# A Strassen tile and shared units of 128, 64 and 32 rows in a top-1 expert layer

## The chip, the cores and the metric

The kernel runs on one core of a Trainium2 chip. The metric is device time in microseconds (us), lower is better. Before the change it is 566.95 us, the median of 3 runs (565.99 to 568.38). The span in the profile, from the first to the last recorded instruction, is shorter (546.6 us), because the launch around it is not in the span.

## The reference

Two blocks follow one another: attention over a band of 96 keys and 8 global ones, and then a layer of 8 experts in which each token goes to the one expert with the highest logit. The change is in the second block alone.

```python
N, D, E, F = (3072, 512, 8, 1024)         # tokens, width, experts, hidden width

def _moe_ref(x, w_gate, w1, w2):
    logits = x @ w_gate
    expert_idx = np.argmax(logits, axis=1)
    ...                                   # gate_w: softmax weight of the chosen expert
    for e in range(E):
        mask = expert_idx == e
        xe = x[mask]
        h = np.maximum(xe @ w1[e], 0.0)   # (rows, 512) @ (512, 1024)
        ye = h @ w2[e]                    # (rows, 1024) @ (1024, 512)
        out[mask] = gate_w[mask, None] * ye
```

All is float32. On the reference's inputs the eight experts get 455, 416, 361, 397, 367, 410, 395 and 271 tokens.

## The kernel before

The attention block scatters each token's row to a region of its expert in DRAM (`xs_dram`); the counts are known only then. `P` is 128, `NDC` = 512/128 = 4, `NFC` = 1024/128 = 8. Every expert is computed in two pieces.

The first 128 rows of an expert are a fixed tile, of one shape for all (`x_in_s` turns the gathered rows with TensorE so that the width lies on the partitions):

```python
def up_s(self, e, half):
    ph = self.turn("ph")                  # a PSUM bank out of three, in turn
    for i in range(NFC // 2):
        f = half * (NFC // 2) + i
        for c in range(NDC):
            nc.tensor.matmul(ph[:, i, :], lhsT=self.w[e % 3][0][:, c, ts(f, P)],
                             rhs=self.xsT[e % 2][:, c, :], start=(c == 0), stop=(c == NDC - 1), ...)
    nc.scalar.activation(self.hsT[...], ph[...], AF.Relu)

def down_s(self, e, half):
    for f in range(half * (NFC // 2), (half + 1) * (NFC // 2)):
        nc.tensor.matmul(py, lhsT=self.hsT[:, f, :], rhs=self.w[e % 3][1][:, f, :], ...)   # 512 columns
    if half:
        nc.vector.tensor_scalar(self.ys[e % 2][:], py, self.gates[:, e:e + 1], None, ALU.mult)
        self.scatter(...)
```

The rows beyond 128 are a pass whose width `n` is a multiple of 16 up to 384. It is chosen by a computed jump (`tc.Switch`) among 18 bodies:

```python
TP = 3
GN = 16
WIDTHS = [0] + list(range(P, TP * P + 1, GN))

def one_pass(self, e, n, between):
    for f in range(NFC if n else 0):
        ph = self.turn("ph")...[:, 0:n]
        for c in range(NDC):
            nc.tensor.matmul(ph, lhsT=w1t[:, c, ts(f, P)], rhs=xT[:, c, 0:n], ...)
        nc.scalar.activation(hT[:, f, 0:n], ph, AF.Relu)
    other()                               # transposes of the next expert's rows
    for d in range(NDC if n else 0):
        py = self.turn("py")...[:, 0:n]
        for f in range(NFC):
            nc.tensor.matmul(py, lhsT=w2t[:, f, ts(d, P)], rhs=hT[:, f, 0:n], ...)
        nc.scalar.copy(self.yT[d % 2][:, 0:n], py)
        if d:
            self.back(e, d - 1, n)        # transposes y back to rows, VectorE scales by the gate
            other()

def passes(self, judge):
    for e in range(E):
        index = {eng: self.forms[e] for eng in self.ENGINES}     # PE, ACT, DVE jump
        for i in tc.Switch(index, len(WIDTHS), hint=f"pass{e}"):
            ...
            self.one_pass(e, WIDTHS[i], more)
        if e + 3 < E: self.fetch(e + 3)   # 4 MB of weights into one of three slots
        ...                               # gathers for later experts
        if e + 1 < E: self.hint(e + 1)    # hints for PE and ACT only (ENGINES[:2])
        ...                               # the fixed tile of expert e + 2, and finish(e)
```

For the eight experts the widths come out as 336, 288, 240, 272, 240, 288, 272 and 144.

Of the kernel before, what the change touches and what calls it, by code (L numbers as in the profile page):

```python
# [9 lines left out]
F32 = mybir.dt.float32  # L10
# [13 lines left out]
def kernel(  # L24
# [227 lines left out]
    def banded(stack, rt, pool, rows, ex, den_all):  # L252
# [195 lines left out]
        for n in range(N + 1):  # L448
# [8 lines left out]
            if n == 2:  # L457
                biases(0, range(H), "act")
                ex.clear_s()
# [271 lines left out]

    NS = 2
    TP = 3
    GN = 16
    WIDTHS = [0] + list(range(P, TP * P + 1, GN))

    class Experts:
        def __init__(self, stack, rt):
# [3 lines left out]
            self.w = [self.slot(self.wpool, i) for i in range(NS)]  # L742
            T = self.pool.tile
            self.pl = T([P, TP], F32, name="pl")
            self.lim = T([P, E], F32, name="lim")
            self.loc = T([P, E, TP], F32, name="loc")
            self.row = T([P, E, TP], F32, name="row")
            self.grow_s = T([P, E], I32, name="grow_s")
            self.inv_s = T([P, E], I32, name="inv_s")
            self.grow = T([P, E, TP], I32, name="grow")  # L750
            self.inv_i = T([P, E, TP], I32, name="inv_i")
            self.form = T([P, E], I32, name="form")
            self.over = T([P, 1], F32, name="over")
            self.xs = [T([P, XW], F32, name=f"xs{i}") for i in range(2)]
# [3 lines left out]
            self.tos = T([P, E], I32, name="tos")  # L758
            self.gates = T([P, E], F32, name="gates")

        def slot(self, pool, i):
            return pool.tile([P, NDC, F], F32, name=f"w1_{i}"), pool.tile([P, NFC, DM], F32, name=f"w2_{i}")

        def fetches(self, e, queue=nc.sync, parts=2):

            w1t, w2t = self.w[e % 3]
            for dst, src, n in ((w1t, moe_w1, NDC), (w2t, moe_w2, NFC)):
                s_ = src[e].rearrange("(c p) f -> p c f", p=P)
                for a in range(0, n, n // parts):
                    r = slice(a, a + n // parts)  # L770
                    yield lambda dst=dst, s_=s_, r=r: queue.dma_start(out=dst[:, r, :], in_=s_[:, r, :])

        def fetch(self, e, queue=nc.sync):
            for load in self.fetches(e, queue):
                load()
# [8 lines left out]
        def scatter(self, src, idx):  # L784
            d = nc.gpsimd.indirect_dma_start(  # L785
                out=out[:], out_offset=bass.IndirectOffsetOnAxis(ap=idx, axis=0),
                in_=src, in_offset=None, bounds_check=NTOK - 1, oob_is_err=False,
            )
            tc.declare_no_dep(d.ins, group="y", reason="every token is in one tile")
            tc.add_to_no_dep_group("y", d.ins)  # L790

        def clear_s(self):
            for t in self.xs:
                nc.gpsimd.memset(t[:], 0.0)
            nc.gpsimd.memset(self.lim[:], float(P))
            nc.gpsimd.iota(self.pl[:], pattern=[[P, TP]], base=0, channel_multiplier=1,
                           allow_small_or_imprecise_dtypes=True)


        def early(self):  # L800
            T = self.pool.tile
            cnt = T([P, NS], F32, name="cnt_s")
            nc.vector.tensor_tensor(cnt[:], self.rt.base_e[:, 0:NS], ebase[:, 0:NS], ALU.subtract)
            nc.vector.tensor_scalar(self.lim[:, 0:NS], cnt[:], float(P), None, ALU.min)
            self.rows_s(cnt, 0, NS)
            shape = [P, E, TP]
            nc.vector.tensor_tensor(self.loc[:], self.pl[:].unsqueeze(1).to_broadcast(shape),
                                    self.lim[:].unsqueeze(2).to_broadcast(shape), ALU.add)
            nc.vector.tensor_tensor(self.row[:], self.loc[:],
                                    ebase[:].unsqueeze(2).to_broadcast(shape), ALU.add)  # L810
            for e in range(NS):
                self.gather_s(e)

        def rows_s(self, cnt, a, b):
            n = b - a
            inv = self.pool.tile([P, n], F32, name=f"inv_s{a}")
            nc.vector.tensor_scalar(inv[:], cnt[:], iota_p[:, 0:1], None, ALU.is_le)
            row = self.pool.tile([P, n], F32, name=f"row_s{a}")
            nc.vector.tensor_scalar(row[:], ebase[:, a:b], iota_p[:, 0:1], None, ALU.add)
            nc.vector.scalar_tensor_tensor(self.grow_s[:, a:b], inv[:], float(2 ** 22), row[:],  # L820
                                           ALU.mult, ALU.add)
            nc.vector.tensor_scalar(self.inv_s[:, a:b], inv[:], float(2 ** 30), None, ALU.mult)

        def gather_s(self, e):
            self.gather(self.xs[e % 2][:], self.grow_s[:, e:e + 1])


        def x_in_s(self, e, pt=None):
            x, pt = self.xs[e % 2], pt or self.turn("t")
            for c in range(NDC):  # L830
                nc.tensor.transpose(pt[:, c, :], x[:, ts(c, P)], ident[:])
            nc.vector.tensor_copy(out=self.xsT[e % 2][:].rearrange("p c t -> p (c t)"),
                                  in_=pt[:].rearrange("p c t -> p (c t)"))
# [4 lines left out]
        def up_s(self, e, half):  # L838
            ph = self.turn("ph")
            for i in range(NFC // 2):  # L840
                f = half * (NFC // 2) + i
                for c in range(NDC):
                    nc.tensor.matmul(ph[:, i, :], lhsT=self.w[e % 3][0][:, c, ts(f, P)],  # L843
                                     rhs=self.xsT[e % 2][:, c, :], start=(c == 0), stop=(c == NDC - 1),
                                     skip_group_check=True)
            nc.scalar.activation(self.hsT[:, half * (NFC // 2):(half + 1) * (NFC // 2), :]
                                 .rearrange("p a b -> p (a b)"), ph[:].rearrange("p a b -> p (a b)"), AF.Relu)

        def down_s(self, e, half):
            if half == 0:  # L850
                self.pys = self.turn("py")
            py = self.pys[:].rearrange("p a b -> p (a b)")
            for f in range(half * (NFC // 2), (half + 1) * (NFC // 2)):
                nc.tensor.matmul(py, lhsT=self.hsT[:, f, :], rhs=self.w[e % 3][1][:, f, :],  # L854
                                 start=(f == 0), stop=(f == NFC - 1), skip_group_check=True)
            if half:
                nc.vector.tensor_scalar(self.ys[e % 2][:], py, self.gates[:, e:e + 1], None, ALU.mult)
                self.scatter(self.ys[e % 2][:], self.tos[:, e:e + 1])


        def begin(self, stack):

            pool = stack.enter_context(tc.tile_pool(name="pass", bufs=1, reuse_waits="tile"))
            self.w.append(self.slot(pool, NS))
            self.xg = [pool.tile([P, TP, XW], F32, name=f"xg{i}") for i in range(2)]
            self.xT = [pool.tile([P, NDC, TP * P], F32, name=f"xT{i}") for i in range(2)]
            self.hT = pool.tile([P, NFC, TP * P], F32, name="hT")
            self.yT = [pool.tile([P, TP * P], F32, name=f"yT{i}") for i in range(2)]
            self.y = [pool.tile([P, TP, DM], F32, name=f"y{i}") for i in range(2)]
            self.to = [pool.tile([P, TP], I32, name=f"to{i}") for i in range(2)]  # L870
            self.gate = [pool.tile([P, TP], F32, name=f"gate{i}") for i in range(2)]
            ps = stack.enter_context(tc.tile_pool(name="ps_e", bufs=1, space=bass.MemoryType.PSUM,
                                                 reuse_waits="tile"))
            self.bank = {nm: [ps.tile([P, 4, P], F32, name=f"{nm}{i}") for i in range(n)]
                         for nm, n in (("ph", 3), ("py", 2), ("t", 3))}
            self.used = {"ph": -1, "py": -1, "t": -1}

        def turn(self, nm):

            self.used[nm] += 1  # L880
            return self.bank[nm][self.used[nm] % len(self.bank[nm])]

        def clear(self, i):
            nc.gpsimd.memset(self.xg[i][:], 0.0)

        def clear_y(self):
            for i in range(2):
                nc.gpsimd.memset(self.y[i][:], 0.0)
                nc.gpsimd.memset(self.yT[i][:], 0.0)

        def table(self):
            T = self.pool.tile
            shape = [P, E, TP]
            cnt = T([P, E], F32, name="cnt")
            nc.vector.tensor_tensor(cnt[:], self.rt.base_e[:], ebase[:], ALU.subtract)
            inv = T(shape, F32, name="inv")
            nc.vector.tensor_tensor(inv[:], self.loc[:], cnt[:].unsqueeze(2).to_broadcast(shape), ALU.is_ge)
            nc.vector.scalar_tensor_tensor(self.grow[:], inv[:], float(2 ** 22), self.row[:],
                                           ALU.mult, ALU.add)
            nc.vector.tensor_scalar(self.inv_i[:], inv[:], float(2 ** 30), None, ALU.mult)  # L900
            self.rows_s(cnt[:, NS:E], NS, E)

            steps = T([P, E], F32, name="steps")
            nc.vector.scalar_tensor_tensor(steps[:], cnt[:], float(GN - 1), self.lim[:],
                                           ALU.add, ALU.subtract)
            steps_i = T([P, E], I32, name="steps_i")
            nc.vector.tensor_scalar(steps_i[:], steps[:], 0.0, None, ALU.max)
            nc.vector.tensor_scalar(steps_i[:], steps_i[:], GN.bit_length() - 1, None,
# [225 lines left out]
```

## Time and profile before

| | before |
|---|---|
| device time, median (range) | 566.95 us (565.99 to 568.38) |
| span in the profile | 546.6 us |
| TensorE (PE) busy | 518.6 us, 95% of the span |
| VectorE (DVE) busy | 170.5 us, 31% |
| ScalarE (ACT) busy | 127.3 us, 23% |
| GpSimd (POOL) busy | 113.9 us, 21% |
| first expert matmul starts | 168.69 us |
| last expert matmul ends | 529.56 us |

An engine's busy time is the time in which at least one of its instructions runs. A group of instructions is listed with its line, engine, operation, operands, shape and count, then busy time and the mean duration of one instruction. One float32 matmul of the program stands in the records as two matmul instructions: `one_pass` has 32 matmuls upwards for each of 8 experts, 256, and the profile counts 512. Matmuls overlap one another, so what one of them costs is read from the distance between starts, not from its duration. "idle" in square brackets is the time in which the engine waited before an instruction, and after the arrow stands what released it; "issue" is a wait for nothing that the profile shows.

### The profile page before, as it was taken

The page shows a single profiled execution, that of the slowest core. Times are in us where ns is not written, and L with a number is a line of the kernel's source. Part 1 is how long each engine was busy: PE and PEld are TensorE (multiplying, and loading weights), DVE is VectorE, ACT ScalarE, POOL GpSimd, SP SyncE. Part 2 cuts the span into 40 slices and gives each one's busy share as a digit, 9 for nine tenths or more (in the row PEclk, how much of TensorE's full clock was granted, in tenths as well). Part 3 has the DMA queues.
Part 4 walks back from the last instruction along what each step waited for, and adds up shares of the span by engine and source line. Part 5 has one row for each costly group of instructions (what it writes and reads, how often), then busy time and mean ns, then how long its engine had stood idle before and what let it go on. Part 6 is the DMA issues. An engine that isn't in the chain of part 4 may idle for free.

```text
span 546.6 us, 11060 instructions
## 1 busy us (share of the span) xinstructions
PE 518.6 (95%) x4544; PEld 428.3 (78%) x4544; DVE 170.5 (31%) x440; ACT 127.3 (23%) x249; POOL 113.9 (21%) x160
## 2 busy tenths in 40 slices
PE   5899999999999999999999999999999999999970
PEld 4798898898988756686787997789699886789940
DVE  5566866866866030110020211011002012011010
ACT  3644455554441001010100201111111210111200
POOL 4200240321334580014002202201400400201020
PEclk9999999999999999999999999999999999999995
DMA  9999999999941493353325246245344200100010
GB/s 173 211 201 207 243 270 240 241 306 240 240 147 40 143 342 112 152 178 113 107 82 189 57 156 214 63 155 177 102 155 154 68 1 7 64 1 31 17 45 7
DMA packets 98378, 77.22 MB, mean 141 GB/s; under 512 B 79290, under 2 KB 79290, under 8 KB 98240
## 3 DMA queue, kind: packets, MB, share of 16 engines
q1 hardware_dynamic: 88768, 52.44, 37.7%
q0 software_dynamic: 7040, 18.99, 10.1%
q10 hardware_dynamic: 2432, 4.21, 2.2%
q8 instruction: 55, 0.90, 0.7%
q14 instruction: 83, 0.68, 0.4%
HBM read 60.90 MB, written 14.73 MB: 138 GB/s over the span
## 4 chain that ended last, share of the span: by engine, by line
PE 73%; issue 18%; DVE 2%; ACT 2%; POOL 2%; DMA 1%; POOLq 0%; SPq 0%; ACTq 0%
PE ph L949 15%; PE py L956 14%; PE ph L843 9%; PE sp L358 8%; PE py L854 8%; PE po L387 7%; PE pt L239 4%; PE pr L398 4%; PE px L417 2%; PE t L927 1%; POOL out_dram L785 1%; DVE p L372 1%; PE pr L403 1%; PE t L970 1%; DMA raw_k<-in_k_dram 1%
## 5 line engine op out<-in xcount | busy, mean ns | idle before, releaser
L956 PE MATMUL py<-hT,w 128*128 128x288 f32 (+4 forms) x512 | 116.2, 383 | 0.0
L949 PE MATMUL ph<-xT,w 128*128 128x288 f32 (+4 forms) x512 | 113.9, 383 | 0.4 <-ACT hT L951 0.4
L949 PEld LDWEIGHTS ph<-xT,w 128*128 128x128 f32 x512 | 92.9, 190 | 22.0 <-issue 2.7
L956 PEld LDWEIGHTS py<-hT,w 128*128 128x128 f32 x512 | 91.5, 190 | 17.6
L973 DVE TENSOR_TENSOR y<-t,gate 128x256 f32<-128x256 f32 (+2 forms) x32 | 13.5, 421 | 148.9 <-PE t L970 106.1
L843 PE MATMUL ph<-xsT,w 128*128 128x128 f32 x512 | 59.7, 275 | 0.0
L843 PEld LDWEIGHTS ph<-xsT,w 128*128 128x128 f32 x512 | 58.4, 192 | 0.5 <-issue 0.5
L372 DVE TENSOR_TENSOR p<-sp,other 128x1024 f32<-128x1024 f32 x40 | 47.1, 1220 | 34.3 <-PE sp L358 32.4
L854 PE MATMUL py<-w,hsT 128*128 128x512 f32 x128 | 56.8, 592 | 0.0
L951 ACT ACTIVATE hT<-ph 128x288 f32<-128x288 f32 (+4 forms) x64 | 24.6, 388 | 130.5 <-PE ph L949 130.5
L785 POOL DMA_INDIRECT out_dram<-y,to x24 | 23.9, 995 | 141.4 <-DVE y L973 136.5
L928 DVE COPY xT<-t 128x512 f32<-128x512 f32 x24 | 15.6, 682 | 111.6 <-PE t L927 111.6
L379 ACT ACTIVATE p<-p 128x1024 f32<-128x1024 f32 (+1 forms) x48 | 44.6, 977 | 2.1 <-DVE p L372 2.0
L854 PEld LDWEIGHTS py<-w,hsT 128*128 128x128 f32 x128 | 23.5, 190 | 25.4 <-issue 25.3
L358 PE MATMUL sp<-qt,kt 64*128 64x128 f32 x448 | 39.0, 281 | 1.2 <-DVE kt L244 1.2
L958 ACT COPY yT<-py 128x288 f32<-128x288 f32 (+4 forms) x32 | 12.0, 376 | 113.5 <-PE py L956 113.5
L387 PE MATMUL po<-p,vt 128*64 128x128 f32 x448 | 37.1, 274 | 0.0
L358 PEld LDWEIGHTS sp<-qt,kt 64*128 64x128 f32 x448 | 31.9, 193 | 3.2 <-ACT qt L242 1.5
L778 POOL DMA_INDIRECT xs<-xs_dram,grow_s x8 | 8.1, 1009 | 118.1 <-issue 90.6
L219 POOL DMA_INDIRECT xs_dram<-xr,slot_i x24 | 23.7, 989 | 20.8 <-DVE base_e L217 9.8
L300 POOL COPY ka<-kt 128x384 f32<-128x384 f32 x16 | 8.2, 512 | 94.0 <-DVE den_all L423 90.9
L387 PEld LDWEIGHTS po<-p,vt 128*64 128x64 f32 x448 | 26.5, 137 | 1.3 <-ACT qt L242 1.2
(157 smaller groups left out, 508.0 us busy)
## 6 DMA issues: line engine op xcount, KB each, us to landing
w<-in_moe_w_dram SPq DMA_DIRECT2D x20, 1024.0 KB, 5.6
w<-in_moe_w_dram SPq DMA_DIRECT2D x16, 512.0 KB, 6.0
raw_q<-in_q_dram SPq DMA_DIRECT2D x24, 256.0 KB, 5.2
raw_k<-in_k_dram SPq DMA_DIRECT2D x24, 256.0 KB, 5.8
vt<-in_v_dram SPq DMA_DIRECT2D x24, 256.0 KB, 5.6
w<-in_moe_w_dram ACTq DMA_DIRECT2D x4, 1024.0 KB, 6.6
va<-vt SPq DMA_DIRECT2D x16, 192.0 KB, 5.6
va<-vt SPq DMA_DIRECT2D x16, 64.0 KB, 5.7
```

What stands on the lines that cost most here:

```text
L219: d = nc.gpsimd.indirect_dma_start(out=xs_dram[:], out_offset=bass.IndirectOffsetOnAxis(ap=slot_i[:, u:u + 1], axis=0), in_=xr[:, u, :].bi ...
L239: nc.tensor.transpose(pt[:, m, :], src[:, 2 * m:2 * m + 2, :].rearrange("p a d -> p (a d)"), ident[:])
L358: nc.tensor.matmul(sp[:, a, j, t, :], lhsT=kt[r, m, :], rhs=qts[n][r, m, :], start=True, stop=True, skip_group_check=True)
L372: nc.vector.tensor_tensor(z, sc, bi, ALU.add)
L379: nc.scalar.activation(z, z, AF.Exp)
L387: nc.tensor.matmul(po[D * a:D * a + D, m, :], lhsT=vt[:, 2 * m + a, :], rhs=ps[n][m // 2][:, a, m % 2, t, :], start=(x == 0), stop=(x == l ...
L785: d = nc.gpsimd.indirect_dma_start(out=out[:], out_offset=bass.IndirectOffsetOnAxis(ap=idx, axis=0), in_=src, in_offset=None, bounds_check ...
L843: nc.tensor.matmul(ph[:, i, :], lhsT=self.w[e % 3][0][:, c, ts(f, P)], rhs=self.xsT[e % 2][:, c, :], start=(c == 0), stop=(c == NDC - 1), ...
L854: nc.tensor.matmul(py, lhsT=self.hsT[:, f, :], rhs=self.w[e % 3][1][:, f, :], start=(f == 0), stop=(f == NFC - 1), skip_group_check=True)
L949: nc.tensor.matmul(ph, lhsT=w1t[:, c, ts(f, P)], rhs=xT[:, c, 0:n], start=(c == 0), stop=(c == NDC - 1), skip_group_check=True)
L951: nc.scalar.activation(hT[:, f, 0:n], ph, AF.Relu)
L956: nc.tensor.matmul(py, lhsT=w2t[:, f, ts(d, P)], rhs=hT[:, f, 0:n], start=(f == 0), stop=(f == NFC - 1), skip_group_check=True)
```

## The change

The work is cut in another way. Experts 0 and 1 keep a fixed tile of 128 rows, which runs while the routing table is made. Then every expert gets one tile of 256 rows. Each of its two products is cut into quarters and done by Strassen's scheme (in Winograd's form): seven products of quarters in place of eight, at the price of sums of quarters. What rows remain are done in units of 128, 64 and 32; the units that are needed are a number `k` from 0 to 7, bit by bit, and a computed jump chooses among 8 bodies. For the eight experts `k` comes out as 3, 1, 4, 5, 4, 5, 5 and 1. Units of 64 and 32 rows use only 64 or 32 columns of TensorE's array, and the kernel puts two or four such products side by side on different columns. The change is for fewer multiplications on TensorE.

The sums of quarters go to VectorE, those of w2 for the larger part to GpSimd, and the copies of half-done sums out of PSUM to ScalarE. Room for the sums comes from the third weight slot, so weights are now held for two experts instead of three, and those of expert e + 2 are fetched at the end of expert e. The down products now have the rows on the output's partitions, so y is no longer transposed back.

The core of the diff (declarations, the routing table and the transposes left out):

```diff
-    TP = 3
-    GN = 16
-    WIDTHS = [0] + list(range(P, TP * P + 1, GN))
+    SP1 = 32
+    FORMS = 8
+    HF = NFC // 2
+    HD = NDC // 2
+    HM = DM // 2
...
+        def combine1(self, e):           # four sums of quarters of w1, 128 x 1024 each
+            yield lambda: nc.vector.tensor_tensor(c[:, 0], a21, a22, ADD)
+            yield lambda: nc.vector.tensor_tensor(c[:, 1], c[:, 0], a11, SUB)
+            yield lambda: nc.vector.tensor_tensor(c[:, 2], a11, a21, SUB)
+            yield lambda: nc.vector.tensor_tensor(c[:, 3], a12, c[:, 1], SUB)
+        def combine_w2(self, e):         # four sums of quarters of w2, 128 x 1024 each
+            c = self.combine2(e)
+            c[2](nc.vector)
+            for i in (0, 1, 3):
+                c[i](nc.gpsimd)
+        def up_a(self, e, j):            # four products of quarters, 128 columns, into bank u[j]
+            for r, lhs, rhs in (...):
+                for k in range(HD):
+                    nc.tensor.matmul(self.u[j][:, r, :], lhsT=lhs(k), rhs=rhs(k), start=first, stop=True, ...)
+        def up_sums(self, j):
+            uv = self.uv[j]
+            nc.scalar.copy(uv[:], self.u[j][:, 0:2, :])
+            nc.vector.tensor_tensor(uv[:], uv[:], self.u[j][:, 2:4, :], ADD)
+            nc.vector.tensor_tensor(self.h[:, j, 3, :], uv[:, 0, :], uv[:, 1, :], ADD)
+            nc.scalar.activation(self.h[:, j, 3, :], self.h[:, j, 3, :], AF.Relu)
+        def up_b(self, e, j):            # the other three products, added into the same bank
+            for r, lhs, rhs in (...):
+                for k in range(HD):
+                    nc.tensor.matmul(self.u[j][:, r, :], lhsT=lhs(k), rhs=rhs(k), start=False, stop=True, ...)
+        def up_end(self, j):             # the hidden rows and the sums of their quarters
+            nc.vector.tensor_tensor(h[:, 1:3, :], ..., b[:, 1:4:2, :], ADD)
+            nc.vector.tensor_scalar(h[:, 0, :], b[:, 0, :], 0.0, None, MAX)
+            nc.scalar.activation(h[:, 2, :], h[:, 2, :], AF.Relu)
+            nc.vector.scalar_tensor_tensor(c[:, 0, :], h[:, 1, :], 0.0, h[:, 3, :], MAX, ADD)
+            nc.vector.tensor_tensor(c[:, 1, :], c[:, 0, :], h[:, 0, :], SUB)
+            nc.vector.scalar_tensor_tensor(c[:, 2, :], h[:, 1, :], 0.0, h[:, 0, :], MAX, SUB)
+            nc.vector.tensor_tensor(c[:, 3, :], h[:, 2, :], c[:, 1, :], SUB)
+        def units(self, e, k):           # the body number k of the jump
+            big, mid, low = k >> 2, k >> 1 & 1, k & 1
+            ...                          # transposes of the units' rows, VectorE copies them to xsT
+            self.up_a(e, 0)
+            self.up_sums(0)
+            ...                          # up products of the units of 64 and 32
+            ...                          # up products of the unit of 128
+            self.up_a(e, 1)
+            self.up_sums(1)
+            ...                          # transposes of the small units' hidden rows
+            self.up_b(e, 0)
+            ...                          # down products of the units, scaled by VectorE
...
         def passes(self, judge):
             for e in range(E):
-                for i in tc.Switch(index, len(WIDTHS), hint=f"pass{e}"):
-                    ...
-                    self.one_pass(e, WIDTHS[i], more)
+                for k in tc.Switch(index, FORMS, hint=f"units{e}"):
+                    self.units(e, k)
+                ...
+                self.up_a(e, 2)
+                self.up_sums(2)
+                self.up_b(e, 1)
+                self.up_end(0)
+                self.up_a(e, 3)
+                self.up_sums(3)
+                self.up_b(e, 2)
+                for j in (1, 2):
+                    self.up_end(j)
+                self.up_b(e, 3)
+                self.up_end(3)
+                self.down_a(e)           # 16 matmuls of 256 columns
+                c1 = list(self.combine1(e + 1)) if more else []
+                for fn in c1[0:3]:
+                    fn()
+                self.down_sums(e)        # ScalarE copies a bank, VectorE adds the other
+                if more:
+                    self.x_in(e + 1)
+                self.down_b(e)           # 12 matmuls of 256 columns
+                self.y_out(e, 1, 1)
+                if more:
+                    self.x_combine()     # four sums of quarters of x, 128 x 256 each
+                    c1[3]()
+                    if e + 2 < E:
+                        self.gather_x(e + 2)
+                        self.fetch(e + 2)
+                self.y_out(e, 0, 1)
+                self.y_out(e, 0, 0)
+                self.y_out(e, 1, 0)
+                if more:
+                    self.combine_w2(e + 1)
+                    self.meta_u(e + 1)
+                for t in range(2):
+                    self.send(e, t)
```

Instructions run in program order on each engine. The order above is therefore also the order of VectorE's queue.

## The prediction, made before the changed kernel ran

> **What bounds the kernel now.** I read first the page's busy times and chain, then the chain in order of time, then VectorE's and ScalarE's timelines around the jumps. From the page:
>
> ```profile
> PE 518.6 (95%) x4544; PEld 428.3 (78%) x4544; DVE 170.5 (31%) x440; ACT 127.3 (23%) x249; POOL 113.9 (21%) x160
> PE 73%; issue 18%; DVE 2%; ACT 2%; POOL 2%; DMA 1%; POOLq 0%; SPq 0%; ACTq 0%
> ```
>
> TensorE is the bound. In the expert part it hardly waits: from 168.69 us (first expert matmul) to 529.56 us (last one's end) are 360.9 us. What a matmul costs I take from the chain of waits in order of time (start, duration, engine, tile, line, count):
>
> ```profile
> 153.78 1.90 PE po L387 x32
> 155.68 1.01 PE pr L398 x32
> ...
> 183.53 7.14 PE ph L843 x64
> 190.67 3.44 PE py L854 x8
> ...
> 216.94 0.87 PE t L927 x8
> 217.81 9.04 PE py L956 x32
> ...
> 300.21 12.96 PE ph L949 x64
> ```
>
> A program matmul is two records. Per record: 128 columns 7.14/64 = 0.1116 us; 512 columns 3.44/8 = 0.430; 240 columns 12.96/64 = 0.2025, hence 256 columns about 0.2025 x 256/240 = 0.216. A transpose 0.87/8 = 0.109. L387 uses half of the array's columns and L398 a quarter: 1.90/32 = 0.059 and 1.01/32 = 0.0316 for 128 columns, 1.9 and 3.5 times as fast as 0.1116. So small products do run side by side.
>
> The other engines have slack, which hides one thing: the jump. ScalarE entering the last pass, and TensorE waiting for it:
>
> ```profile
> 505.40 0.60 ACT L846 ACTIVATE hsT<-ph 128x512 f32<-128x512 f32 x1 [3.30 <-PE ph L843]
> 508.35 0.66 ACT L951 ACTIVATE hT<-ph 128x144 f32<-128x144 f32 x3 [2.35 <-PE ph L949]
> 508.69 0.51 PE L949 MATMUL ph<-xT,w 128*128 128x144 f32 x2 [0.45 <-ACT hT L951]
> ```
>
> Its first Relu was due at about 506.2 (four of the 24 records that start at 505.14 are done by then) and came at 508.35, 2.35 us after ScalarE's last instruction before the jump. VectorE leaving the first pass, while weights arrive:
>
> ```profile
> 238.62 0.16 DVE L934 COPY gate<-xg 128x3 f32<-128x3 f32 x1
> 244.16 0.56 DVE L973 TENSOR_TENSOR y<-t,gate 128x384 f32<-128x384 f32 x1 [5.38 <-issue]
> ```
>
> The transposes it needs started at 241.16, three of them; it came 5.38 us after its last instruction, and none of that is put down to an engine. In 238 to 243 us the weight queue took 100% of the DMA engines. Both waits cost nearly nothing here, since neither engine is near the path.
>
> [...]
>
> **What TensorE saves.** Before, all of it from the rates above. Eight fixed tiles of 4 transposes + 64 records of 128 + 16 of 512: 0.44 + 7.14 + 6.87 = 14.45 us, x8 = 115.6. Eight passes of 128 records, widths summing to 2080, at about 0.00084 us a column and record: 224.6. 96 transposes of x and 87 of y: about 20. Sum 360, which is the 360.9 measured.
>
> After. Main tile per expert: up 7 x 8 = 56 program matmuls of 128 columns, 112 x 0.1116 = 12.5; down 7 x 4 = 28 of 256, 56 x 0.216 = 12.1; 8 transposes 0.87. Sum 25.5, x8 = 203.7. Unit of 128: 14.45, x5 (k = 4, 5, 4, 5, 5) = 72.3. Unit of 32: up 32 records of 256 at 0.216/3.5 = 2.0; down 64 of 128 at 0.0316 = 2.0; transposes 0.5. Sum 4.5, x6 = 27. Unit of 64: 16 records of 512 and 32 of 256, each at 1/1.9, and transposes: 8.1, once. Two fixed tiles 28.9. Sum 340. **TensorE saves 20 us.** That is 3.5%, and all there is to gain: fewer multiplications (256 rows cost 25.5 us and not 28 plus 1 for y's transposes), less what the units round up.
>
> **What goes onto the path.** VectorE gets a queue that must be done between the end of one expert's units and the first small product of the next. Durations: 1024 elements 1.22 (L372); 384 from SBUF 0.56 (L105, L328), so 256 about 0.42 and 128 about 0.29; from PSUM 512 0.68 (L928), 256 0.42 (L973), 128 0.28 (L364). Independent neighbours overlap by 0.08 us. In order:
>
> - last unit's scaling after TensorE, then leaving the jump: 0.45 + 2.35 = 2.8
> - up_sums twice: 1.4; up_end four times (0.42 + 0.28 + four of 0.29 less overlaps = 1.75): 7.0
> - three sums of w1: 3.6; the sum of the two down banks: 0.7
> - copy of the next x with its indices: 0.85; first y quarter 0.4; four sums of x 1.7
> - fourth sum of w1 1.2; three y quarters 1.2; one sum of w2 1.2; unit indices 0.5
> - waits within it on ScalarE's copies and the last down product, estimated from their durations: 0.9
> - entering the jump: 2.35 at least, up to 5 while w2 of expert e + 2 arrives (it starts when the down products have read the slot, 5.6 us to land): 3.5
> - copy of the units' rows: 0.65
>
> Sum 27.6 us. TensorE in the same stretch: two up_a (32 records) and three up_b (36) 68 x 0.1116 = 7.6; down_a 32 x 0.216 = 6.9; transposes of x 0.9; down_b 24 x 0.216 = 5.2; units' transposes 0.7; up_a(0) 1.8. Sum 23.1. So TensorE stands for about 4.5 us per transition, seven times: 31.5. At the first expert the jump alone is in the way (sum of w2, indices, entry and copy, 5.6 us after the last fixed product, against 2.2 us of TensorE work): 3.4. At the last expert down_sums has no transposes to hide behind: 2.5. Sum 37.
>
> GpSimd does three of the four sums of w2, issued next to VectorE's own sum; [...]. At under 1 us a transition I add 5.
>
> What lies beside: fetches (4 MB at 0.38 MB/us in about 11 us, of some 43 us per expert), two weight slots instead of three, the ten gathers and scatters per expert at 1.0 us of GpSimd, and ScalarE's copies. The tail after the last matmul (17 us) stays.
>
> **Sum:** -20 + 37 + 5 = +22, 566.95 + 22 = about 588 us.
>
> **Rivals.** (a) The jumps cost nothing: the bodies are short now (9 or 10 VectorE instructions, 8 bodies), [...]. Then VectorE's queue is 27.6 - 2.35 - 3.5 = 21.8 us against 23.1 and nothing stands: -20 + some 5 of small waits, 550 to 556 us. For it: TensorE's own jumps show no gap. Against it: ScalarE's entry above was hinted, to the third body, and still took 2.35 us. (b) Jumps as reckoned, but the order of the queue works better, with entries free of weight traffic: 2.35 on entry and no hold by GpSimd, 3.3 us a transition, about 573. (c) GpSimd becomes the bound: three sums at perhaps 2 us or more each and ten transfers; its queue is some 20 us of 43, and c2 is needed some 20 us later; little for it, but if it holds VectorE for whole instructions, 605. (d) Column groups don't pair for 256 and 512 columns: a 32-unit would take up to 3.5 times 4 us, 60 us more in all; L387 and L398 speak against it.
>
> **Range and chances.** (a) at 0.25, (b) 0.2, the reckoning 0.4, (c) and (d) the rest. Nothing but (a) comes out below the time before, and only its better half by over 2% (under 555.6 us); same is up to 578.3. So faster 0.14, same 0.24, slower 0.62; 588 us, 558 to 614.
>
> **What would show it.** TensorE's busy time in the expert part near 340 us, plus gaps. The gaps should stand where the first small up product or the first up product of a 128 unit waits for VectorE's copy of the units' rows (xsT), 3 to 6 us once per expert; VectorE should be without idle time from 2 to 3 us after the units' end to there, save a hole of 2.3 us or more on either side of the body. Units of 32 should take 4 to 5 us. I am wrong if TensorE runs through the jumps without a gap (then a), if the gaps are longer at down_b (the sum of banks behind the sums of w1) than at the units, or if the 32 units take over 8 us.

## The result, and the profile after

The changed kernel takes **635.29 us** (median of 4 runs, 635.22 to 638.05), the kernel before beside it 566.53 us: a ratio of **1.122** (95% interval 1.118 to 1.126), 69 us slower. The prediction was 588 us with a range of 558 to 614.

The two profiles cannot be subtracted whole. On one of the chips used here the kernel before takes 549.8 us, on the others 566.5 to 567.2; what differs there is the attention part, which the change does not touch (on that chip, in run 7 below, the first expert matmul starts at 168.9 us, in the changed kernel's profile at 186.2). The profile of before is of an execution of 548.5 us, by its level of the first kind. Its span of 546.6 us is therefore only some 2 us shorter than its time; the 20 us to the median of 566.95 are not the launch. So I compare the experts' part, from the first expert matmul to the last one's end, and the tail after it. TensorE's waits in that part are summed from its list of waits; "running" is the rest.

| | before | after | difference |
|---|---|---|---|
| experts' part | 361.0 us | 427.1 | +66.1 |
| of it, TensorE waits | 0.4 | 65.5 | +65.1 |
| of it, TensorE running | 360.6 | 361.6 | +1.0 |
| tail after the last matmul | 17.0 | 19.5 | +2.5 |
| sum | | | +68.6 |

That is the whole difference. First the page of the changed kernel, the line of busy times:

```profile
PE 528.5 (84%) x5329; PEld 443.3 (70%) x5329; DVE 337.3 (53%) x796; ACT 139.9 (22%) x286; POOL 202.8 (32%) x204
```

TensorE fell from 95% to 84% of the span, and its busy time did not fall. The chain of waits, which carried the reading of before, ends here in GpSimd's last instructions and says nothing. The list of TensorE's waits takes its place (the wait and its releaser; then us in total, times, longest):

```profile
PE u L1144 <- DVE xsT L1135: 31.5, 5, 7.9
PE d L853 <- DVE xsT L1125: 19.9, 2, 12.3
PE t L1124 <- issue: 8.4, 2, 8.1
...
PE u L1023 <- issue: 5.0, 3, 2.9
...
PE u L1041 <- issue: 0.7, 1, 0.7
```

Over 51 us stand where the first product of the units' rows waits for VectorE's copy of those rows, xsT. That is the place that the prediction named. What VectorE does meanwhile shows in the time order of one transition, from expert 0 to expert 1 (start, duration, engine, line, operation, output <- inputs, shapes; in brackets the idle time and what ended it):

```profile
260.61 2.37 POOL L974 TENSOR_TENSOR c<-w 128x1024 f32<-128x1024 f32 x1
...
261.67 1.50 PE L1023 MATMUL u<-cx,c 128*128 128x128 f32 x12
263.06 3.21 POOL L975 TENSOR_TENSOR c<-w,c 128x1024 f32<-128x1024 f32 x1
263.99 2.30 DVE L1106 CAST to_f<-xs 128x3 f32<-128x3 int32 x1
266.33 0.21 DVE L1108 TENSOR_SCALAR to_f<-to_f 128x1 f32<-128x1 f32 x2
266.35 2.34 POOL L977 TENSOR_TENSOR c<-w,c 128x1024 f32<-128x1024 f32 x1
266.58 2.13 DVE L1109 TENSOR_TENSOR to_u<-to_f,inv_u 128x3 int32<-128x3 f32 x1
268.62 0.16 DVE L1110 COPY gate_u<-xs 128x3 f32<-128x3 f32 x1
269.74 0.29 DVE L1135 COPY xsT<-t 128x128 f32<-128x128 f32 x1 [0.96 <-issue]
270.09 3.64 PE L1144 MATMUL u<-w,xsT 128*32 128x256 f32 x32 [6.91 <-DVE xsT L1135]
```

A cast of three elements takes 2.30 us and ends with GpSimd's second sum (266.27); an addition of three elements takes 2.13 and ends with the third. VectorE's own sum of w2 before them takes 2.79 instead of 1.22. Then comes the jump, between gate_u and xsT, with only 0.96 us.

The second thing is the clock. Stretches of the same kernel (from:to, length, busy times and counts of the five engines, granted TensorE clock, DMA share, GB/s); the first has no pause and the third one of 2.9 us, the second and fourth begin after one of 6.9 and one of 12.3 us:

```profile
237.00:260.80 23.80, 23.70 (x207) 21.13 (x203) 16.81 (x45) 4.56 (x12) 6.36 (x6) 1.00 0.54 165
270.10:277.00 6.90, 6.90 (x57) 4.71 (x58) 0.89 (x3) 1.07 (x3) 4.05 (x4) 0.66 0.30 109
277.00:303.30 26.30, 23.37 (x203) 21.39 (x203) 17.04 (x47) 4.87 (x13) 6.21 (x6) 1.00 0.42 137
318.05:330.00 11.95, 11.95 (x87) 11.95 (x88) 0.74 (x3) 1.88 (x4) 2.01 (x2) 0.81 0.03 9
```

Two candidates for the waits, then: **H**, that GpSimd's sums hold VectorE, and **J**, that the jump's entry keeps it from its next instruction. And one for "running": **C**, that every pause is paid a second time by a lower clock.

### The profile page after: what moved, and what is told of

Same layout as the page of the kernel before. It is cut to its first block, busy times and chain, and to the rows that moved or that the text cites. A ratio compares the mean times of both kernels' runs of the same rounds, so it can differ in the third digit from the quotient of the medians.

```text
span 632.8 us, 13136 instructions
## 1 busy us (share of the span) xinstructions
PE 528.5 (84%) x5329; PEld 443.3 (70%) x5329; DVE 337.3 (53%) x796; ACT 139.9 (22%) x286; POOL 202.8 (32%) x204
## 5 line engine op out<-in xcount | busy, mean ns | idle before, releaser
L853 PE MATMUL d<-xsT,w 128*128 128x128 f32 x320 | 42.3, 300 | 19.9 <-DVE xsT L1125 19.9
L853 PEld LDWEIGHTS d<-xsT,w 128*128 128x128 f32 x320 | 41.4, 215 | 22.3 <-DVE xsT L1125 20.3
L785 POOL DMA_INDIRECT xg<-xs_dram,grow x16 | 24.4, 1524 | 88.1 <-issue 84.2
L861 PE MATMUL d<-w,hsT 128*128 128x512 f32 x112 | 49.6, 593 | 0.1
L1023 PE MATMUL u<-cx,c 128*128 128x128 f32 x384 | 48.8, 277 | 0.0
L1066 PE MATMUL d<-c,ch 128*128 128x256 f32 x192 | 46.7, 379 | 0.0
L1023 PEld LDWEIGHTS u<-cx,c 128*128 128x128 f32 x384 | 46.3, 195 | 0.0
L785 POOL DMA_INDIRECT xs<-xs_dram,grow x24 | 24.3, 1014 | 54.1 <-PE d L853 37.1
L1066 PEld LDWEIGHTS d<-c,ch 128*128 128x128 f32 x192 | 36.5, 190 | 5.0
L398 PE MATMUL pr<-p,one_in 128*32 128x128 f32 x704 | 28.5, 278 | 8.7 <-issue 7.9
```

Of the source, the lines that this page charges most:

```text
L398: nc.tensor.matmul(pr[GW * m:GW * m + GW, 0, :], lhsT=one_in[:, a, :], rhs=ps[n][m // 2][:, a, m % 2, t, :], start=(x == 0), stop=False, s ...
L785: nc.gpsimd.indirect_dma_start(out=dst.bitcast(I32), out_offset=None, in_=xs_dram[:], in_offset=bass.IndirectOffsetOnAxis(ap=idx, axis=0), ...
L853: nc.tensor.matmul(ph[:, i, :], lhsT=self.w[e % 2][0][:, c, ts(half * HF + i, P)], rhs=xT[:, c, :], start=(c == 0), stop=(c == NDC - 1), s ...
L861: nc.tensor.matmul(py[:].rearrange("p a b -> p (a b)"), lhsT=self.hsT[:, f, :], rhs=self.w[e % 2][1][:, f, :], start=(f == 0), stop=(f == ...
L1023: nc.tensor.matmul(self.u[j][:, r, :], lhsT=lhs(k), rhs=rhs(k), start=first, stop=True, skip_group_check=True)
L1066: nc.tensor.matmul(self.half(i, j), lhsT=lhs, rhs=rhs, start=(f == 0 and j == 0), stop=True, skip_group_check=True)
```

## The experiments

Differences are to the kernel before on the same chip. The expectations give times for a chip on which the kernel before takes 566.5 us; runs 5 to 8 came onto the one where it takes 549.8, so their differences are what to compare. The time of run 7 leaves out one of its four executions (882.37 us at a granted clock of 0.56), and the profile of run 6 is of an execution of 553.29 us, 1.6% above its fastest.

### 1. GpSimd's sums left out

For experts 1 to 7 the three sums of w2 on GpSimd are not computed, so the output is not the reference's.

```diff
-            for i in (0, 1, 3):
+            for i in (0, 1, 3) if e == 0 else ():
                 c[i](nc.gpsimd)
```

> GpSimd's three sums of w2 are left out for experts 1 to 7 (its output is then not the reference's; all else as in the changed kernel). Theory H (GpSimd's sums hold VectorE): the sum of w2, the cast and the index sum on VectorE fall from 2.8, 2.3 and 2.1 us to 1.22, 0.16 and 0.15, so each of the seven waits of TensorE between experts is about 5.9 us shorter (41 us in all), the granted clock no longer falls after them (up to 20 us more): about 578 us. Theory J (the jumps): the holds are beside the point, 625 to 635. Theory Q (VectorE's queue is too long by its own work, as predicted): some 3 to 5 us of wait stay per transition, 590 to 600.

Measured: 619.91 us, ratio 1.092 (1.088 to 1.097). The same transition in its time order:

```profile
261.35 1.22 DVE L976 TENSOR_TENSOR c<-w 128x1024 f32<-128x1024 f32 x1
...
262.48 0.16 DVE L1106 CAST to_f<-xs 128x3 f32<-128x3 int32 x1
...
262.93 0.16 DVE L1109 TENSOR_TENSOR to_u<-to_f,inv_u 128x3 int32<-128x3 f32 x1
263.01 0.42 DVE L1110 COPY gate_u<-xs 128x3 f32<-128x3 f32 x1
268.11 0.29 DVE L1135 COPY xsT<-t 128x128 f32<-128x128 f32 x1 [4.68 <-issue]
```

The hold is real: 2.79, 2.30 and 2.13 became 1.22, 0.16 and 0.16, 5.7 us less. But the copy comes only 1.7 us earlier, reckoned from VectorE's sum of w2 (6.76 us after its start, 8.47 in the changed kernel), since the jump's entry now shows 4.68 us where it had shown 0.96. The two had run side by side. In the whole experts' part the waits fall from 65.5 to 46.7 us, but running grows from 361.6 to 365.1. H alone falls as the explanation of the 69 us.

### 2. The sends of y ahead of the sums

```diff
-                    self.combine_w2(e + 1)
+                    sums = self.combine_w2(e + 1)
                     self.meta_u(e + 1)
                 for t in range(2):
                     self.send(e, t)
+                if more:
+                    sums()               # GpSimd's three sums
```

> The same sums, but GpSimd sends y first and sums then, so that the sums run beside the units, when VectorE has little to do. H: nearly all of what leaving them out brings, about 580 us. J: 635, as the changed kernel. If GpSimd itself is too slow for the later order, the first down product with c2 waits for it and the time stays over 600.

Measured: 625.10 us, 1.102 (1.100 to 1.105). The waits in the experts' part fell from 65.5 to 53.8 us. A change of place alone brings 10 us.

### 3. All sums of w2 on VectorE

```diff
-            c[2](nc.vector)
-            for i in (0, 1, 3):
-                c[i](nc.gpsimd)
+            for i in (2, 0, 1, 3):
+                c[i](nc.vector)
```

> All four sums of w2 on VectorE, none on GpSimd. H: 3.7 us more of work in VectorE's queue per transition against 5.9 us of hold: each wait some 2 us shorter, 610 to 620 us. If the length of the queue alone counts (Q) and the hold doesn't: 7 x 3.7 more, about 661. J: about 635.

Measured: 639.61 us, 1.126 (1.121 to 1.131). VectorE's own three sums cost what the hold had cost (waits 65.8 us): at the same transition they take 3.7 us and the entry shows 2.92, where the changed kernel had 5.7 of hold and 0.96.

### 4. The unit bodies laid down, no jump

The numbers of the bodies for this input are written into the program, so it serves this input alone; the arithmetic stays.

```diff
-                for k in tc.Switch(index, FORMS, hint=f"units{e}"):
+                for k in ((3, 1, 4, 5, 4, 5, 5, 1)[e],):
                     self.units(e, k)
```

> No jump: each expert's units are laid down in the program for these inputs (3, 1, 4, 5, 4, 5, 5, 1), hints left out. H: the pauses before the units stay, less about 1 us of entry each and about 6 us of TensorE's waits on leaving (2.9, 2.0, 0.7) and 3.5 at the third expert: 610 to 620 us. J (jumps cost 2.35 us or more on either side, as predicted): 2.35 + 3.5 us per transition less, 33 us and the clock's losses with them: 580 to 595.

Measured: 617.56 us, 1.091 (1.089 to 1.093). The transition again:

```profile
263.91 2.13 DVE L1109 TENSOR_TENSOR to_u<-to_f,inv_u 128x3 int32<-128x3 f32 x1
265.96 0.16 DVE L1110 COPY gate_u<-xs 128x3 f32<-128x3 f32 x1
266.03 0.28 DVE L1135 COPY xsT<-t 128x128 f32<-128x128 f32 x1
...
266.37 3.64 PE L1144 MATMUL u<-w,xsT 128*32 128x256 f32 x32 [5.85 <-DVE xsT L1135]
```

Without the jump the copy follows at once, and TensorE still waits 5.85 us: the hold is untouched. One line of this run's list of TensorE's waits:

```profile
PE t L1124 <- DVE bad_i L1277: 8.0, 1, 8.0
```

It explains a wait that the changed kernel showed only as "issue" (8.09 us): the units' transposes write a PSUM bank in which a tally of the rows' validity has just been added up, and VectorE, held, has not read it. J alone falls too.

### 5. and 6. No jump and no hold

Run 5 joins edits 2 and 4, run 6 edits 1 and 4 (sums left out again).

> The unit bodies are laid down as in the run without a jump, and the sends of y are issued ahead of GpSimd's sums, so both causes are taken away together. [...] the waits before the units and after them shrink from 65 us to under 20 us and the time is 555 to 568 us. If something third (the length of the queue itself, the scheme's additions) holds TensorE, waits of 3 to 4 us a transition stay and the time is 580 to 600 us.

> No jump, and GpSimd's three sums of the third matrix left out for experts 1 to 7 (the output is then not the reference's). If hold and jump together are the cause, 550 to 562 us, a little under the run with the sends first, since nothing holds VectorE anywhere. If the queue's own length is the cause, 575 to 595 us. If leaving the sums out and putting them later come to the same time within 1%, only their place in time matters, not their work.

Measured: run 5 577.21 us, 27 over before, 1.048 (1.043 to 1.052); run 6 549.94 us, 0.997 (0.994 to 1.001). By its number run 5 points to a third cause. Its time order at the same transition does not:

```profile
250.10 2.91 DVE L1108 TENSOR_TENSOR to_u<-to_f,inv_u 128x3 int32<-128x3 f32 x1
...
250.61 2.38 POOL L974 TENSOR_TENSOR c<-w 128x1024 f32<-128x1024 f32 x1
252.94 0.15 DVE L1109 COPY gate_u<-xs 128x3 f32<-128x3 f32 x1
253.01 0.28 DVE L1134 COPY xsT<-t 128x128 f32<-128x128 f32 x1
...
253.34 1.93 PE L1143 MATMUL u<-w,xsT 128*32 128x256 f32 x32 [2.91 <-DVE xsT L1134]
```

The sums only moved by some instructions and now hold the last addition ahead of the copy. In run 6, where they are gone, the same product waits 0.26 us, and the waits of the experts' part are 10.5 us in all. So the four runs make a square: jump and hold +69 us, hold alone +51, jump alone +53, neither none that can be measured. Each hides most of the other. (Runs 1 and 6 also leave out the sums' work; runs 8, 10 and 11 below keep it.)

### 7. The copies of the units' rows on ScalarE

```diff
-                nc.vector.tensor_copy(out=self.xsT[0][:], in_=self.t[0][:])
+                nc.scalar.copy(self.xsT[0][:], self.t[0][:])
...
-                nc.vector.tensor_copy(out=xm[:, :, r], in_=self.t[1][:, :, r])
+                nc.scalar.copy(xm[:, :, r], self.t[1][:, :, r])
```

> Only the two copies of the units' rows out of PSUM go from VectorE to ScalarE; the jump and GpSimd's sums stay as in the changed kernel. If TensorE waits because these copies stand behind the jump in VectorE's held queue, the waits before the units that begin with the gate products fall from 5 to 12 us to under 2 us each and the time is 570 to 585 us. If every engine is late at the jump alike [...], waits of 4 to 5 us stay and the time is 610 to 625 us.

Measured: 567.46 us (median of three) where before takes 549.84: 1.034 (1.028 to 1.039), 18 us over before instead of 69. Jump and hold are all still there:

```profile
238.28 0.27 ACT L1135 COPY xsT<-t 128x128 f32<-128x128 f32 x1 [4.33 <-PE t L1131]
...
240.07 1.93 PE L1144 MATMUL u<-w,xsT 128*32 128x256 f32 x32
...
240.97 2.31 DVE L1106 CAST to_f<-xs 128x3 f32<-128x3 int32 x1
...
246.73 0.42 DVE L1030 TENSOR_TENSOR uv<-uv,u 128x256 f32<-128x256 f32 x1 [0.96 <-issue]
```

ScalarE had been idle for 4.33 us when the rows came; it jumped early and copied at once. VectorE is as late as ever (246.73), and TensorE goes on past it. Two lines of code took away 50 us: what hurt was whose queue the copy stood in. The changed kernel was not run on this chip, but the experts' parts of the two profiles, which leave the attention part out, say the same: waits fall from 65.5 to 25.9 us and running from 361.6 to 350.7. The waits left (25.9 us) are the tally's bank (8.1), the small units' hidden rows and sums behind VectorE (11.7), and TensorE's own leaving of bodies (about 5).

### 8. Copies on ScalarE, sends first, the tally in another bank

```diff
-                pb = ex.t[0][:].rearrange("p t c -> p (t c)")
+                pb = ex.u[1][:].rearrange("p t c -> p (t c)")
```

(beside edits 2 and 7.)

> The copies on ScalarE, the sends ahead of GpSimd's sums, and the tally of the third expert's part taken in another PSUM bank than the one that the units' transposes need; the jump stays. If hold and VectorE's late entry are the cause, this comes near the kernel without a jump: 558 to 572 us. [...]

Measured: 558.65 us, 1.015 (1.010 to 1.020), 9 us over before, a little worse than expected. Of the 16.8 us of waits left one of 5.3 us is VectorE's tally (11 instructions, two of them held for 2.2 us each) between a pass and the next units.

### 9. to 12. The tally early, everything fixed, and pauses put back

Run 9 is the changed kernel once more. Run 10 is run 8 with the tally moved; run 11 is run 10 with edit 4; run 12 is run 10 with idle copies on ScalarE ahead of each jump.

```diff
                 self.up_end(3)
+                if e in (2, 3):
+                    judge(e - 1)         # runs 10 to 12
                 self.down_a(e)
...
                 if more:
+                    for _ in range(20):  # run 12 alone
+                        nc.scalar.copy(self.xsT[0][:], self.xsT[0][:])
                     sums()
-                if e in (1, 2):
-                    judge(e)
```

> The changed kernel itself, unaltered, beside the others on their chip. If only the attention part differs from chip to chip, the difference to the kernel before is about 69 us here too, whatever the level. If the lower clock after pauses belongs to a chip, the difference is smaller on a chip whose attention part runs at full clock: 65 us of waits + 2.5 of tail - 12 of saved work = 55 to 60 us.

> Copies on ScalarE and sends ahead of the sums, as in the run that combined them, and the tally (20 small VectorE instructions and one product) moved from the end of the second and third expert's pass to the middle of the third's and fourth's, after the last product of w1. It had cost one wait of 5.3 us. Expected 4 to 6 us less than that run: a ratio to the kernel before of 1.00 to 1.01. If VectorE has no room in the middle either, the wait turns up at the products of w2 and nothing is gained.

> The same with the unit bodies laid down, no jump at all: every known cause is gone. If nothing else holds TensorE, its waits in the experts' part are under 6 us and the ratio is 0.985 to 0.995, which is the saving of work (some 12 us) less the longer tail (2.5 to 3 us) and is what the scheme is worth here. A ratio above 1.01 would mean a cause that is not found yet.

> As the run with the early tally, with 20 idle copies on ScalarE (about 12 us) at the end of each of seven passes, so that TensorE waits some 6 to 9 us for the units' rows at each transition while everything else stays. If the clock granted after a pause is lower, the time grows by more than the sum of TensorE's new waits, by 10 to 20 us over seven transitions, and the clock falls to 0.94 to 0.96. If pauses cost only themselves, growth and waits agree within 4 us and the clock of the stretches that run stays at 0.98 or more.

| | time | ratio (95%) | waits | running |
|---|---|---|---|---|
| 9 changed again | 636.29 us | 1.122 (1.117 to 1.127) | 64.3 us | 362.3 us |
| 10 tally early | 567.11 | 1.000 (0.998 to 1.002) | 10.8 | 346.4 |
| 11 no jump as well | 561.71 | 0.990 (0.987 to 0.993) | 5.3 | 347.3 |
| 12 pauses put back | 642.17 | 1.132 (1.128 to 1.137) | 72.4 | 361.4 |

The kernel before took 567.17 us there. Run 9 is a repeat and no more: its chip was again one with the longer attention part, so whether the 69 us are fewer on the other kind was not tried.

The tally is 11 instructions, not the 20 of my expectation. Run 10 computes all that the changed kernel does, for any input, and is 69 us faster: it ties with the kernel before. Run 11, for this input alone, is 1% under it. Runs 10 to 12 settle C. The whole experts' part of run 10, with the columns of the stretches above:

```profile
187.40:544.60 357.20, 346.00 (x2675) 289.47 (x2673) 204.64 (x511) 62.01 (x161) 155.39 (x115) 1.00 0.35 113
```

And of run 12:

```profile
186.90:620.70 433.80, 361.11 (x2675) 298.85 (x2673) 197.60 (x511) 148.39 (x301) 155.10 (x115) 0.91 0.29 93
```

The same 2675 matmul records take 346 us at a clock of 1.00 and 361 at 0.91. The pauses added 61.6 us of waits, and the running grew by 15.0 beside them. Where it grows, shows in two products of run 12 in its time order:

```profile
267.18 3.64 PE L1143 MATMUL u<-w,xsT 128*32 128x256 f32 x32 [9.11 <-ACT xsT L1134]
...
312.14 9.43 PE L853 MATMUL d<-xsT,w 128*128 128x128 f32 x64 [9.61 <-ACT xsT L1124]
```

The like in run 10, without a pause before them:

```profile
258.53 1.93 PE L1143 MATMUL u<-w,xsT 128*32 128x256 f32 x32
...
295.10 7.31 PE L853 MATMUL d<-xsT,w 128*128 128x128 f32 x64
```

The first loses 1.7 us; the second, of four times the length, 2.1 (another of its kind 2.9). The low clock ended while TensorE worked: in the changed kernel it was 0.66 in the 6.9 us behind one pause and 1.00 in the 26.3 us that followed, and 0.81 in the 12 us behind another and 1.00 in the 28 us after those.

## Why the prediction was wrong

**TensorE's saving: there, but 14 us and not 20.** I reckoned 360 us before and 340 after; undisturbed it is 360.6 and 346 to 347. Six us are missing. In run 10, by the distance of starts, a quarter product of 128 columns costs 0.1154 us a record and not 0.1116, 3.4 us over 896 records. The unit of 64 took 7.2 us besides its few transposes, which is as reckoned; the rest is spread over the other products. The small products run side by side as reckoned (32 records of 256 columns in 1.93 us, 64 of 128 in 1.95; 2.0 each was said). Rival (d) is out.

**The place: right.** The gaps stand before the first product of the units' rows. At the last expert's sum of banks, where I had 2.5 us, no gap stands; the tail is longer by 2.5 us instead, which I had said stays.

**GpSimd's hold: the first step that failed.** I wrote "under 1 us a transition, I add 5". It is 5.7 us at six of the seven transitions (VectorE's sum of w2 +1.57, the cast +2.14, the addition +1.97) and about 3 at the last. My 5 us were a guess, worked out from no reading: I thought that the trace of before had no case. It has one, beside a GpSimd instruction that only writes: a copy of three elements that takes 0.15 to 0.16 us for the seven other experts took 1.93 here, and ended with GpSimd's clearing of a tile:

```profile
196.46 1.93 DVE L934 COPY gate<-xg 128x3 f32<-128x3 f32 x1
...
196.60 1.40 POOL L888 MEMSET y<- 128x1536 f32 x1
...
197.92 0.44 POOL L889 MEMSET yT<- 128x384 f32 x1
```

My own rival put GpSimd's sums at "perhaps 2 us or more each", and they take 2.3 to 3.2; three in a row stand right beside VectorE's last instructions before the copy. Rival (c) was the right mechanism, and I gave it almost no weight. But this step alone would not have saved the number. In run 1 the hold is gone for seven experts and the kernel is still 53 us over before, where my terms without the hold give 17: the waits are 46.7 us and not 37, and running is 365.1 us against run 10's 346.4, at a clock of 0.93 against 1.00.

**The entry of the jump: of the right size, wrongly added.** 3.5 us were reckoned; alone, in run 1, it is 3.1 to 5.4 at the transitions (4.68 at the one shown) and, under the hold, 0.96 there. So a transition is not 4.5 plus the hold, but 4.5 + 5.7 - 2.5 (the part of the 3.5 that the hold covers) = 7.7 us, and the five transitions without the tally measure 6.1 to 7.9. (The head, at the first expert, is 4.0 against 3.4 reckoned, but by luck: an entry of 0.85 us, and a hold of 2.8 that I had not put there.) The rest of VectorE's queue was about right: with neither jump nor hold it holds TensorE for 0.2 to 0.3 us at the four transitions that begin with a small product (run 6), and my numbers without the two entries, 21.8 us against 23.1, say none.

**Left out: the tally and TensorE's own exits.** I did not reckon the tally's instructions, which lengthen one transition to 12.35 us, nor its PSUM bank, which makes another 8.09. TensorE leaves a body with nothing to do for up to 2.9 us, 5.0 in all; I had said its jumps show no gap.

**Left out: the clock, the second step that failed.** The waits that I added (42 us with the 5 for the hold) were pauses of some 5 us, and pauses of that length cost more than themselves in these runs. In the changed kernel running takes 361.6 us instead of run 10's 346.4: 15.2 us over eight pauses of more than 3.5 us, 1.9 us each. The small product of 32 records shows where it lies: directly after pauses of 0.2 to 3.1 us it takes 1.93 us (runs 4 to 6), and 3.2 to 3.64 after every pause from 3.5 us upward (the changed kernel, runs 1 to 4 and 12). But that is no sharp limit, and shorter pauses are not always free. In run 11 a pause of 1.96 us was followed by a clock of 0.50 (the second line is a stretch as above), and groups of four quarter-product records (L1040) that elsewhere take 0.61 us took 1.06:

```profile
514.59 0.45 PE L1154 MATMUL t<-ident,hr 128*128 128x128 f32 x2 [1.96 <-ACT hr L1146]
...
514.90:518.20 3.30, 3.30 (x30) 3.03 (x32) 1.75 (x3) 0.31 (x1) 2.85 (x3) 0.50 0.04 8
```

In run 5 the small product took 1.93 us, as without a pause, after all four pauses of 2.9 to 3.1 us before it. What decides between the two, these runs do not show.

The sum, by the measured terms: -14.2 of work, +65.1 of waits, +15.2 of clock, +2.5 of tail = +68.6; the prediction had -20, +42, 0 and 0.

## What to carry to other kernels

Before handing a second engine work "that runs beside", look at what the first engine does in those microseconds and whether TensorE waits behind it: with the same hold no wait stands before the first product of the units' rows where the copy is ScalarE's (run 7, where the cast still takes 2.31 us), and 5.85 us stand there where the copy comes straight after it on VectorE (run 4). Give the copy that releases the next product to an engine that is idle by then; the two moved lines were worth 50 of the 69 us. And reckon with more than the length of a wait: each TensorE wait of 3.5 us or more cost about 2 us beside itself here, in the mean (1.9 in the changed kernel, 2.1 in run 12).

## What the runs showed that I had not expected

- Two causes that hide each other: taking either away alone brings 16 to 18 us, both together 69. One such run by itself would have put either cause at a quarter of the loss.
- An instruction of three elements was held longer than one of 1024: the cast took 2.30 us instead of 0.16 and ended with GpSimd's sum, and VectorE's own sum 2.79 instead of 1.22. The two in-place tensor_scalar instructions of one element behind the cast, begun at 266.33 as GpSimd's third sum began at 266.35, took 0.21 us together.
- Pauses alone, made by ScalarE while hold and late VectorE stand off the path as in run 10, bring back the whole loss (run 12, 642 us): it hangs on the pauses, and not on which of the two engines makes them.
- At best the scheme gains 1% here (run 11): of 20 us reckoned, 13 to 14 are there on TensorE, and the tail and small waits take more than half of them.
